# Windowed attention block on one core: row maxima on the full array, narrower score strips, and a deferred Q/K split

## The chip, the cores and the metric

The kernel runs on one core of one Trainium2 chip. The metric is the device time of one execution in microseconds; the median of the runs shown is compared. A core has TensorE (PE, with its weight loads shown as PEld), VectorE (DVE), ScalarE (ACT), GpSimd (POOL) and SyncE (SP, which issues nearly all transfers here). Each engine works off its own queue in order; the queues meet at semaphores.

## The reference, cut to what matters

The program computes one transformer block on a [2048, 640] input: a layer norm, sliding-window attention, and a gated MLP whose gate mixes over positions. Only the attention matters here.

```python
B, S, D = x.shape
H = 32; Dh = D // H; W = 256
qkv = (lambda x, *d: x.transpose(*d))((x @ wqkv).reshape(B, S, 3, H, Dh), 2, 0, 3, 1, 4)
q, k, v = qkv[0], qkv[1], qkv[2]
scores = jnp.einsum("bhqd,bhkd->bhqk", q, k) * (Dh ** -0.5)
idx = jnp.arange(S)
mask = (idx[:, None] - idx[None, :] >= 0) & (idx[:, None] - idx[None, :] < W)
scores = jnp.where(mask[None, None], scores, -1e9)
p = _softmax(scores, axis=-1)
o = jnp.einsum("bhqk,bhkd->bhqd", p, v)
```

A query sees itself and the 255 positions before it. The softmax needs each row's maximum, so the kernel computes the scores twice: once with queries on partitions, to take the maxima, and once with keys on partitions, for the exponentials.

## The kernel before, in words

**Tiles and stages.** The 2048 positions are 16 tiles of 128; the 32 heads are 8 groups g of 4 heads hh. The order of work on PE, DVE and ACT is the order in which the Python code emits it (manual schedule, lines 38-39). POOL and SP are placed by the framework's scheduler at build time, from the dependencies.

**Norm and V** (lines 463-485): for 16 tiles, load, normalise, transpose, and multiply for V. The normalisation takes two short POOL instructions (lines 75, 76) between its DVE steps. Before it, POOL fills constants: `mask` (lines 220-223) and `strip` (224-231), the additive masks of the maxima.

**Q and K** (lines 486-499): `qk_item(m, c)` makes 128 rows of Q/K for 512 positions: 15 matmuls of 512 columns (lines 434-436) into one of two PSUM banks, with a `yield` after every third. Then it splits the result into three bf16 pieces: ACT copies (440), DVE subtracts (441), ACT copies (442), POOL subtracts (443), and SP writes the pieces to `qk_d` in DRAM (446). Of 40 items 24 run back to back. `load_stack(g)` reads a group's pieces back into one of three slots; the pieces lie on the contraction axis, 120 rows deep.

**Lead** (lines 501-530): the other 16 items are drawn out of the generator `dense` three matmuls at a time (a dense step), and between them stand the maxima of group 0 (64 items) and of the first four query tiles of group 1 (16 items).

**`max_item(g, qb, hh)`** (lines 267-285) takes one of three PSUM banks (tag s1) and fills it with four matmuls side by side, each 32 queries (a strip) against the 288 keys that these 32 can see; for qb < 2 all four go against the first 128 or 256 keys. Then one fused DVE operation (284) adds the mask, reduces by max into a column of `mcol`, and writes the sums that nobody reads to `junk`, a bf16 tile of which there are two buffers. On the chip it is two DVE instructions: the reduction, and a read of the accumulator, which signals the end of the item. Ahead of the reduction stands a wait on DVE's own semaphore as an instruction of its own; the wait for PE is part of the reduction. `max_rows(g)` (287-299) turns a finished group's maxima with PE, splits them on DVE (292-296), and sends them through DRAM into the slot, as three rows more of Q.

**Attention steps** (lines 535-567): for s from 0 to 129 and hh from 0 to 3, in this order: the `max_item` 20 units ahead (while s < 108), the `score_item` of unit s, and, after hh = 2, `pv_item(s - 2)`. A unit is one group and one tile of 128 keys.

**`score_item`** (lines 317-341), while s <= 108, takes one of three PSUM banks (tag s2): four matmuls side by side, 32 keys each against the 384 queries from the tile's first on. ACT exponentiates the 384 columns into `pt` (335). After the fourth head POOL zeroes what lies outside the window: the triangle in the first 128 columns (337), that in the last 128 (340). From s = 109 on, items are two heads wide. `pv_item` (343-371) multiplies `pt` with V; every fourth unit a finished bank is copied out, by ACT (366) in most of the stage.

**The rest**: the output projection, and the MLP (lines 574-1105), which the change doesn't touch.

Of the kernel before, what the change touches and what calls it, by code (L numbers as in the profile page):

```python
# [7 lines left out]
F32 = mybir.dt.float32  # L8
F32R = mybir.dt.float32r
BF16 = mybir.dt.bfloat16  # L10
AF = mybir.ActivationFunctionType
OP = mybir.AluOpType
# [3 lines left out]
P = 128  # L16
# [11 lines left out]
NEG = -3.0e38  # L28
# [6 lines left out]
def block_kernel(ctx, tc, x, wqk, wv, wo, w_in, wsp, bsp, w_out, out):  # L35
    nc = tc.nc
# [4 lines left out]
    def pool(stack, name, **kw):  # L41
# [17 lines left out]
                            compare_op=OP.is_equal, fill=0.0)  # L59
# [138 lines left out]
    with ExitStack() as ab:  # L198
# [15 lines left out]
        def add_slot(i, flat):  # L214
# [2 lines left out]

        add_slot(0, slot0)
        add_slot(2, xb[:, :4 * S])
        mask = tmp2.tile([P, 256], BF16, name="mask")  # L220
        nc.gpsimd.memset(mask, 0.0)
        nc.gpsimd.affine_select(out=mask, in_=mask, pattern=[[-1, 256]], base=128, channel_multiplier=1,
                                compare_op=OP.is_ge, fill=NEG)
        strip = tmp2.tile([P, 288], BF16, name="strip")
        nc.gpsimd.memset(strip, 0.0)
        for j in range(4):
            m = strip[32 * j:32 * j + 32]
            nc.gpsimd.affine_select(out=m, in_=m, pattern=[[1, 288]], base=-1, channel_multiplier=-1,
                                    compare_op=OP.is_ge, fill=NEG)
            nc.gpsimd.affine_select(out=m, in_=m, pattern=[[-1, 288]], base=256, channel_multiplier=1,  # L230
                                    compare_op=OP.is_ge, fill=NEG)
        v_sb = vpool.tile([P, NT, VW], F32, name="v_sb")
        nc.gpsimd.memset(v_sb[:, :, 672:VW], 0.0)
        v4 = v_sb[:, :, :672].rearrange("p t (h c) -> p t h c", c=21)
# [2 lines left out]
        LEAD = 20  # L237
# [2 lines left out]
        psB = ab.enter_context(ExitStack())  # L240
        ps6 = [pool(psB, "ps6", space=PSUM)]

        def s1_tile(name):
            return ps6[0].tile([P, 512], F32, tag="s1", bufs=3, name=name)

        def s2_tile(name):
            return ps6[0].tile([P, 512], F32, tag="s2", bufs=3, name=name)

        def pv_tile(name):
            return psA.tile([P, 512], F32, tag="pv", bufs=2, name=name)  # L250
# [13 lines left out]
                    nc.sync.dma_start(st[j:6 * DH:6, a], src)  # L264
                    yield

        def max_item(g, qb, hh):

            st = slot_ap[g % 3]
            ps = s1_tile(f"sm{g}_{qb}_{hh}")  # L270
            if qb < 2:
                n, keep = (qb + 1) * P, mask[:, 256 - (qb + 1) * P:]
            else:
                n, keep = 288, strip
            for j in range(4):
                q0 = qb * P + 32 * j
                k0 = 0 if qb < 2 else q0 - 256
                nc.tensor.matmul(ps[32 * j:32 * j + 32, :n], st[:120, 0, hh, q0:q0 + 32], st[:120, 1, hh, k0:k0 + n],  # L278
                                 start=True, stop=True, tile_position=(0, 32 * j))
            if qb == 0 and hh == 0:  # L280
                m_cols[g] = tmp2.tile([P, 64], F32, tag="mcol", bufs=2, name=f"mcol{g}")
            junk = tmp2.tile([P, 288], BF16, tag="junk", bufs=2, name=f"junk{g}_{qb}_{hh}")
            c = hh * 16 + qb
            nc.vector.tensor_tensor_reduce(out=junk[:, :n], in0=ps[:, :n], in1=keep, scale=1.0,  # L284
                                           scalar=NEG, op0=OP.add, op1=OP.max, accum_out=m_cols[g][:, c:c + 1])
# [30 lines left out]

        def score_item(u, hh, width):

            g, kb = divmod(u, NT)
            st = slot_ap[g % 3]  # L320
            n = min(384, S - kb * P)
            if hh == 0:
                p_tiles[u] = tmp3.tile([P, 4, 384], F32, tag="pt", bufs=4, name=f"pt{u}")
            pt = p_tiles[u]
            if width == 1:
                ps = s2_tile(f"st{u}_{hh}")[:, None, :]
            else:
                ps = ps6[0].tile([P, 2, 512], F32, tag="sp", bufs=3, name=f"st{u}_{hh}")
            for j in range(width):
                for i in range(4):  # L330
                    k0 = kb * P + 32 * i
                    nc.tensor.matmul(ps[32 * i:32 * i + 32, j, :n], st[:123, 1, hh + j, k0:k0 + 32],  # L332
                                     st[:123, 0, hh + j, kb * P:kb * P + n], start=True, stop=True,
                                     tile_position=(0, 32 * i))
            nc.scalar.activation(pt[:, hh:hh + width, :n], ps[:, :, :n], AF.Exp, scale=SCALE)  # L335
            if hh + width == 4:
                nc.gpsimd.affine_select(out=pt[:, :, :P], in_=pt[:, :, :P], pattern=[[0, 4], [1, P]], base=0,  # L337
                                        channel_multiplier=-1, compare_op=OP.is_ge, fill=0.0)
                if n == 384:
                    nc.gpsimd.affine_select(out=pt[:, :, 256:], in_=pt[:, :, 256:], pattern=[[0, 4], [-1, P]],  # L340
                                            base=-1, channel_multiplier=1, compare_op=OP.is_ge, fill=0.0)
# [32 lines left out]
        if True:  # L374
# [26 lines left out]
            def vgemm(i):  # L401
                c, o = divmod(i, 4)
                t0 = o * P
                for j in range(2):
                    ps = (s1_tile if j else pv_tile)(f"v{i}_{j}")
                    n0 = j * HD
                    for k in range(KD):
                        hi, lo = xn_hi[c][:, k, t0:t0 + P], xn_lo[c][:, k, t0:t0 + P]
                        wh, wl = wv_hi[:, k, n0:n0 + HD], wv_lo[:, k, n0:n0 + HD]
                        nc.tensor.matmul(ps[:, :HD], hi, wh, start=(k == 0), stop=False)  # L410
                        nc.tensor.matmul(ps[:, :HD], hi, wl, start=False, stop=False)
                        nc.tensor.matmul(ps[:, :HD], lo, wh, start=False, stop=(k == KD - 1))
                    nc.scalar.activation(v4[:, i, 16 * j:16 * j + 16, :DH],
                                         ps[:, :HD].rearrange("p (h c) -> p h c", c=DH), AF.Copy)

            wqs, raws = {}, {}

            def load_wqk(m):
                raws[m] = tmp.tile([P, KD, P], F32, tag="wraw", bufs=5, name=f"wqraw{m}")
# [10 lines left out]
            def qk_item(m, c):  # L430
                ps = pv_tile(f"qk{m}_{c}")
                hi, lo = wqs[m]
                for k in range(KD):
                    nc.tensor.matmul(ps, hi[:, k, :], xn_hi[c][:, k, :], start=(k == 0), stop=False)
                    nc.tensor.matmul(ps, hi[:, k, :], xn_lo[c][:, k, :], start=False, stop=False)
                    nc.tensor.matmul(ps, lo[:, k, :], xn_hi[c][:, k, :], start=False, stop=(k == KD - 1))
                    yield
                sg = tmp.tile([P, 3, 512], BF16, tag="ta", bufs=3, name=f"sg{m}_{c}")
                rest = tmp.tile([P, 512], F32, tag="tb", bufs=2, name=f"rest{m}_{c}")
                nc.scalar.activation(sg[:, 0, :], ps, AF.Copy)  # L440
                nc.vector.tensor_tensor(out=rest, in0=ps, in1=sg[:, 0, :], op=OP.subtract)  # L441
                nc.scalar.activation(sg[:, 1, :], rest, AF.Copy)  # L442
                nc.gpsimd.tensor_tensor(out=sg[:, 2, :], in0=rest, in1=sg[:, 1, :], op=OP.subtract)  # L443
                T = S // 2
                base = qk_d[m // 5, 0, m % 5 * 8, 0, c * 256:(c + 1) * 256]
                nc.sync.dma_start(bass.AP(tensor=base.tensor, offset=base.offset,
                                          ap=[[T, P], [2 * DH * H // 2 * T, 3], [1, 256]]), sg.bitcast(F32))
# [23 lines left out]
            for i in range(NT):  # L471
                if i + 3 < NT:
                    load_x(i + 3)
                if i + 2 < NT:
                    ln1(i + 2)
                if i == 0:
                    vgemm(0)
                if i + 1 < NT:
                    turn1(i + 1)
                if i >= NT - 6 and i < NT - 2:  # L480
                    load_wqk(i - (NT - 6))
                if i >= NT - 3:
                    split_wqk(i - (NT - 3))
                if i:
                    vgemm(i)
            ld0, ld1 = load_stack(0), load_stack(1)
            for m in range(6):
                for c in range(4):
# [26 lines left out]
                next(dense, None)  # L515
            for u in range(16):
                for hh in range(4):
                    max_item(0, u, hh)
                    if hh < 3:
                        next(dense, None)  # L520
            max_rows(0)
            for u in range(LEAD - 16):
                for hh in range(4):
                    if u:
                        max_item(1, u - 1, hh)
                    next(dense, None)
            for hh in range(4):
                max_item(1, LEAD - 17, hh)
            for _ in dense:
                pass  # L530

        b1.close()
# [565 lines left out]
    n = NT - 2  # L1098
# [34 lines left out]
```

## Time and profile before

| | us |
|---|---|
| median of three runs | 1188.22 (1185.37 to 1189.32) |
| the profiled execution | 1185.69 |
| its span, first to last instruction | 1184.0 |
| PE busy | 1126.5 |
| DVE busy | 738.8 |
| ACT busy | 537.6 |
| POOL busy | 391.5 |

The span is what the trace covers; the profiled execution's own time is 1.7 us longer. Busy times count stretches in which an engine has at least one instruction under way; matmuls are pipelined, so a busy PE can still be a waiting one. The line numbers of the profile are those of the kernel above. In the tables, the columns after the count (x) are the busy time, the mean duration of one instruction, and the idle time of the engine just before such instructions with what ended it. Two instructions of an engine can overlap in the trace: what an instruction costs is then the distance from its start to the next start, which is shorter than its duration.

### The profile page before, as it was taken

How to read it: one execution, taken by the hardware profiler on the slowest of the kernel's cores; microseconds unless marked ns; L12 is line 12 of the kernel's file. 1: busy time of each engine (PE TensorE's matmuls, PEld its weight loads, DVE VectorE, ACT ScalarE, POOL GpSimd, SP SyncE). 2: the span in 40 equal slices, each digit the busy share in tenths (PEclk: the TensorE clock that was granted, in tenths of full speed). 3: DMA queues.
4: the chain of work that ended last, by engine and by line, in shares of the span. 5: the costliest groups of instructions: out<-in, count | busy, mean ns of one | idle time of the engine just before them, and what ended most of it. 6: DMA issues, size and time to landing. Idle time of an engine off the chain costs nothing. (4 is left out here: it accounts for less than half of the span.)

```text
span 1184.0 us, 26538 instructions
## 1 busy us (share of the span) xinstructions
PE 1126.5 (95%) x10272; PEld 963.8 (81%) x10272; DVE 738.8 (62%) x1949; ACT 537.6 (45%) x1121; POOL 391.5 (33%) x485
## 2 busy tenths in 40 slices
PE   5999999999999999878899999899999899999998
PEld 5998886546666666468899999799999889999998
DVE  5541123658888888559967658755548985656443
ACT  3333433228888888834446655433335531221110
POOL 4123443336556555845722036100015530000000
PEclk9999999999999999989999999899999999999999
DMA  6212453543444441558845441133331364444322
GB/s 191 77 34 89 143 195 138 187 150 114 173 166 175 174 175 42 188 174 289 270 156 189 174 134 36 36 132 131 120 139 57 125 193 152 129 140 136 86 87 82
DMA packets 72125, 165.20 MB, mean 140 GB/s; under 512 B 9128, under 2 KB 33448, under 8 KB 70056
## 3 DMA queue, kind: packets, MB, share of 16 engines
q1 hardware_dynamic: 69696, 158.27, 40.1%
q10 hardware_dynamic: 2304, 5.24, 1.1%
q8 instruction: 80, 1.31, 0.5%
q14 instruction: 45, 0.37, 0.1%
HBM read 108.83 MB, written 54.66 MB: 138 GB/s over the span
## 5 line engine op out<-in xcount | busy, mean ns | idle before, releaser
L335 ACT ACTIVATE pt<-st 128x384 f32<-128x384 f32 (+2 forms) x474 | 199.0, 513 | 34.8 <-PE st L332 27.3
L284 DVE CUSTOM_DVE_ANT_0 junk<-sm,strip 128x288 bf16<-128x288 f32 x448 | 181.0, 454 | 50.8 <-PE sm L278 49.6
L930 PE MATMUL g<-zl,aw 128*128 128x432 f32 x768 | 173.6, 361 | 7.2 <-ACT zl L598 4.9
L598 ACT ACTIVATE aw<-fx 128x512 fp32r<-128x512 f32 (+2 forms) x160 | 92.9, 596 | 185.7 <-PE g L930 120.9
L930 PEld LDWEIGHTS g<-zl,aw 128*128 128x128 f32 x768 | 144.6, 189 | 15.3 <-ACT zl L598 5.7
L930 PE MATMUL g<-ze,aw 128*128 128x432 f32 x576 | 137.0, 365 | 4.1 <-DVE row L592 1.8
L592 DVE TENSOR_TENSOR aw<-fx,aw 128x512 fp32r<-128x512 f32 (+2 forms) x152 | 108.4, 722 | 36.2 <-ACT aw L598 36.0
L930 PEld LDWEIGHTS g<-ze,aw 128*128 128x128 f32 x576 | 108.8, 192 | 11.6 <-ACT aw L598 1.7
L332 PE MATMUL st<-slot 123*32 123x384 bf16 (+2 forms) x1536 | 110.6, 318 | 6.6 <-ACT pt L335 3.6
L337 POOL TENSOR_SCALAR_AFFINE_SELECT pt<-pt 128x512 f32<-128x512 f32 x128 | 82.1, 642 | 90.9 <-ACT pt L335 90.9
L278 PE MATMUL sm<-slot 120*32 120x288 bf16 (+2 forms) x1536 | 109.1, 284 | 3.2 <-DVE mcol L284 2.5
L356 PE MATMUL pv<-pt,v_sb 128*32 128x384 f32 (+2 forms) x1408 | 102.7, 384 | 3.0 <-POOL pt L340 1.9
L969 PE MATMUL out_ps<-wout,y_sp 128*128 128x320 f32 (+1 forms) x630 | 96.2, 309 | 0.4 <-ACT y_sp L122 0.4
L834 PE MATMUL zb<-win,aw 128*128 128x432 f32 x480 | 95.3, 359 | 0.0
L969 PEld LDWEIGHTS out_ps<-wout,y_sp 128*128 128x128 f32 (+1 forms) x630 | 94.1, 188 | 1.2 <-ACT y_sp L122 0.7
L834 PEld LDWEIGHTS zb<-win,aw 128*128 128x128 f32 x480 | 89.9, 187 | 4.7
L278 PEld LDWEIGHTS <-slot 120*32 120x32 bf16 x1536 | 49.2, 95 | 42.6 <-issue 35.0
L332 PEld LDWEIGHTS <-slot 123*32 123x32 bf16 x1536 | 50.4, 96 | 38.3 <-issue 19.3
L441 DVE TENSOR_TENSOR rest<-qk,sg 128x512 f32<-128x512 f32 x40 | 27.7, 691 | 86.3 <-ACT sg L440 86.0
L443 POOL TENSOR_TENSOR sg<-rest,sg 128x512 bf16<-128x512 f32 x40 | 46.5, 1163 | 98.7 <-ACT sg L442 96.2
L340 POOL TENSOR_SCALAR_AFFINE_SELECT pt<-pt 128x512 f32<-128x512 f32 x112 | 73.9, 660 | 0.0
L592 DVE TENSOR_TENSOR row<-g,row 128x432 f32<-128x432 f32 x80 | 48.1, 604 | 36.0 <-PE g L930 32.3
(172 smaller groups left out, 2092.8 us busy)
## 6 DMA issues: line engine op xcount, KB each, us to landing
slot<-qk_d SPq DMA_DIRECT2D x72, 320.0 KB
fx<-wsp_in SPq DMA_DIRECT2D x32, 512.0 KB
qk_d<-sg SPq DMA_DIRECT2D x40, 384.0 KB
fx<-hn_d SPq DMA_DIRECT2D x32, 320.0 KB
o_d<-ot SPq DMA_DIRECT2D x32, 256.0 KB
xb<-qk_d SPq DMA_DIRECT2D x24, 320.0 KB
z_d<-row SPq DMA_DIRECT2D x16, 432.0 KB
g_d<-row SPq DMA_DIRECT2D x16, 432.0 KB
```

What stands on the lines that cost most here:

```text
L278: nc.tensor.matmul(ps[32 * j:32 * j + 32, :n], st[:120, 0, hh, q0:q0 + 32], st[:120, 1, hh, k0:k0 + n], start=True, stop=True, tile_positi ...
L284: nc.vector.tensor_tensor_reduce(out=junk[:, :n], in0=ps[:, :n], in1=keep, scale=1.0, scalar=NEG, op0=OP.add, op1=OP.max, accum_out=m_cols ...
L332: nc.tensor.matmul(ps[32 * i:32 * i + 32, j, :n], st[:123, 1, hh + j, k0:k0 + 32], st[:123, 0, hh + j, kb * P:kb * P + n], start=True, sto ...
L335: nc.scalar.activation(pt[:, hh:hh + width, :n], ps[:, :, :n], AF.Exp, scale=SCALE)
L337: nc.gpsimd.affine_select(out=pt[:, :, :P], in_=pt[:, :, :P], pattern=[[0, 4], [1, P]], base=0, channel_multiplier=-1, compare_op=OP.is_ge ...
L340: nc.gpsimd.affine_select(out=pt[:, :, 256:], in_=pt[:, :, 256:], pattern=[[0, 4], [-1, P]], base=-1, channel_multiplier=1, compare_op=OP. ...
L356: nc.tensor.matmul(ps[32 * hh:32 * hh + 32, a - 512 * c:b - 512 * c], v_sb[:, kb, v0:v0 + 32], pt[:, hh, a - kb * P:b - kb * P], start=fir ...
L592: (eng or nc.vector).tensor_tensor(out=out, in0=a, in1=b, op=op)
L598: nc.scalar.activation(out, a, AF.Copy)
L834: nc.tensor.matmul(b[0][:, :HF], a[t][:, x, kk], win2[0][:, y, kk, h * HF:(h + 1) * HF], start=kk + x + y == 0, stop=kk == KD - 1 and x == 1)
L930: nc.tensor.matmul(ps, w[m][:, x, k], zc[k][m][:, y], start=start and k + x + y == 0, stop=stop and k == 3 and x == 1, skip_group_check=True)
L969: nc.tensor.matmul(ps[j][:, :HD], src[:w, a, k, :], e1["wout"][:w, b, k, j * HD:(j + 1) * HD], start=(k == 0 and a + b == 0), stop=(k == K ...
```

## The change

- **Maxima.** `max_item` gets a flag. In the lead it is off, and a query tile from the third on is one matmul of 128 queries against 384 keys on the full array, in place of four strips of 288; the first two tiles are one matmul too, of 128 and 256 keys. In the attention steps the flag is on: the third tile and later ones keep the strips, the first two are one matmul. `mask` grows to 384 columns, with a second select for the window's far edge. `junk` grows to 384 columns and has one buffer in place of two.
- **Strip mask.** The code that builds `strip` moves from ahead of the norms to behind the V stage.
- **Scores.** The three score banks become fixed tiles that are taken in turn. An item that is one head wide computes, for each strip of 32 keys, the 288 queries that can see them and not all 384. ACT still reads 384 columns: what lies outside a strip's 288 is left from earlier uses of the bank, and the selects of lines 337 and 340 zero it.
- **Q/K split.** `qk_item` ends with the first ACT copy only. The DVE subtraction is emitted after the first three matmuls of the next item, the rest of the split after the second three; the last item's remainder after the last maxima of the lead.

```diff
@@ -217,18 +217,13 @@

         add_slot(0, slot0)
         add_slot(2, xb[:, :4 * S])
-        mask = tmp2.tile([P, 256], BF16, name="mask")
+        mask = tmp2.tile([P, 384], BF16, name="mask")
         nc.gpsimd.memset(mask, 0.0)
-        nc.gpsimd.affine_select(out=mask, in_=mask, pattern=[[-1, 256]], base=128, channel_multiplier=1,
+        nc.gpsimd.affine_select(out=mask, in_=mask, pattern=[[1, 384]], base=-1, channel_multiplier=-1,
+                                compare_op=OP.is_ge, fill=NEG)
+        nc.gpsimd.affine_select(out=mask, in_=mask, pattern=[[-1, 384]], base=256, channel_multiplier=1,
                                 compare_op=OP.is_ge, fill=NEG)
         strip = tmp2.tile([P, 288], BF16, name="strip")
-        nc.gpsimd.memset(strip, 0.0)
-        for j in range(4):
-            m = strip[32 * j:32 * j + 32]
-            nc.gpsimd.affine_select(out=m, in_=m, pattern=[[1, 288]], base=-1, channel_multiplier=-1,
-                                    compare_op=OP.is_ge, fill=NEG)
-            nc.gpsimd.affine_select(out=m, in_=m, pattern=[[-1, 288]], base=256, channel_multiplier=1,
-                                    compare_op=OP.is_ge, fill=NEG)
         v_sb = vpool.tile([P, NT, VW], F32, name="v_sb")
         nc.gpsimd.memset(v_sb[:, :, 672:VW], 0.0)
         v4 = v_sb[:, :, :672].rearrange("p t (h c) -> p t h c", c=21)
@@ -240,11 +235,14 @@
         psB = ab.enter_context(ExitStack())
         ps6 = [pool(psB, "ps6", space=PSUM)]

+        s2s, s2n = [ps6[0].tile([P, 512], F32, name=f"s2_{i}") for i in range(3)], [0]
+
         def s1_tile(name):
             return ps6[0].tile([P, 512], F32, tag="s1", bufs=3, name=name)

         def s2_tile(name):
-            return ps6[0].tile([P, 512], F32, tag="s2", bufs=3, name=name)
+            s2n[0] += 1
+            return s2s[s2n[0] % 3]

         def pv_tile(name):
             return psA.tile([P, 512], F32, tag="pv", bufs=2, name=name)
@@ -264,22 +262,26 @@
                     nc.sync.dma_start(st[j:6 * DH:6, a], src)
                     yield

-        def max_item(g, qb, hh):
+        def max_item(g, qb, hh, strips=True):

             st = slot_ap[g % 3]
             ps = s1_tile(f"sm{g}_{qb}_{hh}")
-            if qb < 2:
-                n, keep = (qb + 1) * P, mask[:, 256 - (qb + 1) * P:]
+            lo = max(0, qb - 2) * P
+            n = (qb + 1) * P - lo
+            if strips and qb > 1:
+                n, keep = 288, strip
+                for j in range(4):
+                    q0 = qb * P + 32 * j
+                    nc.tensor.matmul(ps[32 * j:32 * j + 32, :n], st[:120, 0, hh, q0:q0 + 32],
+                                     st[:120, 1, hh, lo + 32 * j:lo + 32 * j + n], start=True, stop=True,
+                                     tile_position=(0, 32 * j))
             else:
-                n, keep = 288, strip
-            for j in range(4):
-                q0 = qb * P + 32 * j
-                k0 = 0 if qb < 2 else q0 - 256
-                nc.tensor.matmul(ps[32 * j:32 * j + 32, :n], st[:120, 0, hh, q0:q0 + 32], st[:120, 1, hh, k0:k0 + n],
-                                 start=True, stop=True, tile_position=(0, 32 * j))
+                keep = mask[:, 384 - n:]
+                nc.tensor.matmul(ps[:, :n], st[:120, 0, hh, qb * P:(qb + 1) * P], st[:120, 1, hh, lo:lo + n],
+                                 start=True, stop=True)
             if qb == 0 and hh == 0:
                 m_cols[g] = tmp2.tile([P, 64], F32, tag="mcol", bufs=2, name=f"mcol{g}")
-            junk = tmp2.tile([P, 288], BF16, tag="junk", bufs=2, name=f"junk{g}_{qb}_{hh}")
+            junk = tmp2.tile([P, 384], BF16, tag="junk", bufs=1, name=f"junk{g}_{qb}_{hh}")
             c = hh * 16 + qb
             nc.vector.tensor_tensor_reduce(out=junk[:, :n], in0=ps[:, :n], in1=keep, scale=1.0,
                                            scalar=NEG, op0=OP.add, op1=OP.max, accum_out=m_cols[g][:, c:c + 1])
@@ -329,8 +332,9 @@
             for j in range(width):
                 for i in range(4):
                     k0 = kb * P + 32 * i
-                    nc.tensor.matmul(ps[32 * i:32 * i + 32, j, :n], st[:123, 1, hh + j, k0:k0 + 32],
-                                     st[:123, 0, hh + j, kb * P:kb * P + n], start=True, stop=True,
+                    b, e = (32 * i, min(n, 32 * i + 288)) if width == 1 else (0, n)
+                    nc.tensor.matmul(ps[32 * i:32 * i + 32, j, b:e], st[:123, 1, hh + j, k0:k0 + 32],
+                                     st[:123, 0, hh + j, kb * P + b:kb * P + e], start=True, stop=True,
                                      tile_position=(0, 32 * i))
             nc.scalar.activation(pt[:, hh:hh + width, :n], ps[:, :, :n], AF.Exp, scale=SCALE)
             if hh + width == 4:
@@ -413,7 +417,7 @@
                     nc.scalar.activation(v4[:, i, 16 * j:16 * j + 16, :DH],
                                          ps[:, :HD].rearrange("p (h c) -> p h c", c=DH), AF.Copy)

-            wqs, raws = {}, {}
+            wqs, raws, after = {}, {}, [iter(())]

             def load_wqk(m):
                 raws[m] = tmp.tile([P, KD, P], F32, tag="wraw", bufs=5, name=f"wqraw{m}")
@@ -434,11 +438,21 @@
                     nc.tensor.matmul(ps, hi[:, k, :], xn_hi[c][:, k, :], start=(k == 0), stop=False)
                     nc.tensor.matmul(ps, hi[:, k, :], xn_lo[c][:, k, :], start=False, stop=False)
                     nc.tensor.matmul(ps, lo[:, k, :], xn_hi[c][:, k, :], start=False, stop=(k == KD - 1))
+                    if k < 2:
+                        next(after[0], None)
                     yield
+                for _ in after[0]:
+                    pass
+                after[0] = split_qk(m, c, ps)
+                next(after[0])
+
+            def split_qk(m, c, ps):
                 sg = tmp.tile([P, 3, 512], BF16, tag="ta", bufs=3, name=f"sg{m}_{c}")
                 rest = tmp.tile([P, 512], F32, tag="tb", bufs=2, name=f"rest{m}_{c}")
                 nc.scalar.activation(sg[:, 0, :], ps, AF.Copy)
+                yield
                 nc.vector.tensor_tensor(out=rest, in0=ps, in1=sg[:, 0, :], op=OP.subtract)
+                yield
                 nc.scalar.activation(sg[:, 1, :], rest, AF.Copy)
                 nc.gpsimd.tensor_tensor(out=sg[:, 2, :], in0=rest, in1=sg[:, 1, :], op=OP.subtract)
                 T = S // 2
@@ -483,6 +497,13 @@
                     split_wqk(i - (NT - 3))
                 if i:
                     vgemm(i)
+            nc.gpsimd.memset(strip, 0.0)
+            for j in range(4):
+                m = strip[32 * j:32 * j + 32]
+                nc.gpsimd.affine_select(out=m, in_=m, pattern=[[1, 288]], base=-1, channel_multiplier=-1,
+                                        compare_op=OP.is_ge, fill=NEG)
+                nc.gpsimd.affine_select(out=m, in_=m, pattern=[[-1, 288]], base=256, channel_multiplier=1,
+                                        compare_op=OP.is_ge, fill=NEG)
             ld0, ld1 = load_stack(0), load_stack(1)
             for m in range(6):
                 for c in range(4):
@@ -515,18 +536,20 @@
                 next(dense, None)
             for u in range(16):
                 for hh in range(4):
-                    max_item(0, u, hh)
+                    max_item(0, u, hh, False)
                     if hh < 3:
                         next(dense, None)
             max_rows(0)
             for u in range(LEAD - 16):
                 for hh in range(4):
                     if u:
-                        max_item(1, u - 1, hh)
+                        max_item(1, u - 1, hh, False)
                     next(dense, None)
             for hh in range(4):
-                max_item(1, LEAD - 17, hh)
+                max_item(1, LEAD - 17, hh, False)
             for _ in dense:
+                pass
+            for _ in after[0]:
                 pass

         b1.close()
```

## The prediction, made blind

> **What bounds the kernel now.** I read the page first, then the busy times by stage, then single stretches of the timeline.
>
> ```profile
> span 1184.0 us, 26538 instructions
> ...
> L284 DVE CUSTOM_DVE_ANT_0 junk<-sm,strip 128x288 bf16<-128x288 f32 x448 | 181.0, 454 | 50.8 <-PE sm L278 49.6
> ```
>
> ```profile
> core 0: us, PE busy (x) PEld busy (x) DVE busy (x) ACT busy (x) POOL busy (x), PEclk, DMA share, GB/s
> 90.00:193.20 103.20, 102.70 (x457) 83.80 (x456) 18.68 (x27) 39.28 (x65) 47.22 (x36) 1.00 0.44 151
> 193.20:265.60 72.40, 70.42 (x518) 36.75 (x518) 42.60 (x176) 15.96 (x26) 21.25 (x15) 1.00 0.45 154
> 265.60:475.00 209.40, 200.54 (x4630) 133.77 (x4622) 176.08 (x890) 180.80 (x458) 124.52 (x203) 1.00 0.40 144
> ```
>
> The rows are the Q/K items, the lead, and the 108 attention steps with maxima. PE is all but full in the first two. In the third, DVE (176 of 209 us), ACT (181) and PE (201) are all close to the wall: a step takes 209.4 / 108 = 1.94 us, and whatever makes one of the three slower by a fifth becomes the bound. One step, on PE:
>
> ```profile
> 365.06 0.35 PE L332 MATMUL st<-slot 123*32 123x384 bf16 x4
> 365.23 0.31 PE L278 MATMUL sm<-slot 120*32 120x288 bf16 x4
> 365.35 0.35 PE L332 MATMUL st<-slot 123*32 123x384 bf16 x4
> 365.53 0.31 PE L278 MATMUL sm<-slot 120*32 120x288 bf16 x4
> 365.71 0.35 PE L332 MATMUL st<-slot 123*32 123x384 bf16 x4
> 365.87 0.84 PE L356 MATMUL pv<-pt,v_sb 128*32 128x256 f32 x16
> 366.52 0.31 PE L278 MATMUL sm<-slot 120*32 120x288 bf16 x4
> ```
>
> Read the distances of the starts: a group of score strips (384 columns) costs 0.17 us, a group of maxima strips (288) 0.12, the product with V 0.65. That is 1.80 a step; the rest are waits, as at 365.71, 0.06 late.
>
> **The one buffer of `junk`** is the part that decides. Before, maxima run back to back on DVE like this:
>
> ```profile
> 264.49 0.45 DVE L284 CUSTOM_DVE_ANT_0 junk<-sm,strip 128x288 bf16<-128x288 f32 x1
> 264.87 0.08 DVE L284 DVE_READ_ACCUMULATOR2_ANT mcol<- 128x1 f32 x1
> 264.87 0.45 DVE L284 CUSTOM_DVE_ANT_0 junk<-sm,strip 128x288 bf16<-128x288 f32 x1
> 265.25 0.08 DVE L284 DVE_READ_ACCUMULATOR2_ANT mcol<- 128x1 f32 x1
> ```
>
> An item costs 0.38 us: the next reduction starts together with the accumulator read of the last one. That is possible because, with two buffers, the wait in front of a reduction is for the accumulator read of the item before the last. In the changed program as built, the count waited for is one higher: the accumulator read of the very last item. The wait instructions are there already, so nothing new shows in an instruction count:
>
> ```profile
> L284 DVEq EVENT_SEMAPHORE  x496: 21/21/21, 194.6 to 473.9; - x166
> ```
>
> Now the parts follow each other. The accumulator read starts when the reduction is through, with a follower or without:
>
> ```profile
> 249.30 0.46 DVE L284 CUSTOM_DVE_ANT_0 junk<-sm,strip 128x288 bf16<-128x288 f32 x1 [0.66 <-PE sm L278]
> 249.69 0.08 DVE L284 DVE_READ_ACCUMULATOR2_ANT mcol<- 128x1 f32 x1
> 250.16 0.28 DVE L292 TENSOR_SCALAR m<-mt 64x128 bf16<-64x128 f32 x1 [0.39 <-PE mt L289]
> 250.48 0.28 DVE L293 SCALAR_TENSOR_TENSOR mr<-mt,m 64x128 f32<-64x128 f32 x1
> ```
>
> So 0.39 and 0.08, and then the way over the semaphore. Its price is not shown for this instruction. From below: L293 waits for L292 on the same engine and starts 0.04 after its end (250.16 + 0.28 to 250.48), with the wait inside the instruction. The wait here stands alone, as it does ahead of L441:
>
> ```profile
> 112.85 0.60 ACT L440 ACTIVATE sg<-qk 128x512 bf16<-128x512 f32 x1 [1.46 <-PE qk L436]
> ...
> 113.55 0.69 DVE L441 TENSOR_TENSOR rest<-qk,sg 128x512 f32<-128x512 f32 x1 [2.82 <-ACT sg L440]
> ```
>
> From the end of L440 (113.45) to L441 are 0.10. That is the nearest row, and I take it: 0.39 + 0.08 + 0.10, **0.57 us an item**; by the lower price it would be 0.51. Four items make 2.28 us a step. PE then needs 4 x 0.12 + 4 x 0.12 + 0.65 = 1.6, ACT 180.8 / 108 = 1.7, POOL 1.2: DVE alone sets the step, and the columns saved on PE buy nothing. The three banks hide nothing, as they only let PE run ahead of DVE.
>
> A rule of the Trainium skill speaks against this: VectorE: DVE Perf Modes, section "The DRAIN you can't avoid", measured the same time for eight copies with a semaphore after each as with one after the last, and says that the semaphore costs nothing extra, since the next operation waits for an empty pipe anyhow. By it an item would stay at 0.38 us. The rows at 264.49 disagree as far as they go: a reduction recorded at 0.45 is followed after 0.38, so there is an overlap that a wait can take away.
>
> The other widths come from one row of the view of `junk`:
>
> ```profile
> L284 DVE CUSTOM_DVE_ANT_0 junk<-sm,mask x64: 275/354/427, 193.5 to 447.1; 128x128 bf16<-128x128 f32 x32, 128x256 bf16<-128x256 f32 x32
> ```
>
> The shortest is 128 wide, the longest 256. Less the 0.07 of overlap, plus 0.19 for read and wait (0.57 - 0.38): 0.40 and 0.54; at 0.14 per 128 columns, 0.67 for 384. The steps hold 48 items of group 1 and six groups of 64 (4 of 0.40, 4 of 0.54, 56 of 0.57, which is 35.7) with a `max_rows` of 1.2 each (250.16 on, four operations): 27.4 + 6 x 36.9 = 248.7 us on DVE, without a gap. They take 209.4 now: **+39.3**.
>
> **The lead.** PE, where a single item stands between dense steps, and one round of four items and three dense steps:
>
> ```profile
> 200.74 0.40 PE L436 MATMUL qk<-xa,wql 128*128 128x512 f32 x1
> 201.07 0.31 PE L278 MATMUL sm<-slot 120*32 120x288 bf16 x4
> 201.30 0.50 PE L434 MATMUL qk<-xa,wqh 128*128 128x512 f32 x1
> 201.64 0.40 PE L435 MATMUL qk<-xa,wqh 128*128 128x512 f32 x1
> 201.88 0.40 PE L436 MATMUL qk<-xa,wql 128*128 128x512 f32 x1
> ...
> 204.59 0.31 PE L278 MATMUL sm<-slot 120*32 120x288 bf16 x4
> ```
>
> Dense matmuls follow after 0.24. The item adds 0.33 + 0.23 + 0.34 - 2 x 0.24 = 0.42, though its columns take 0.12: going into strips and out of them costs 0.1 each way. That agrees with the Trainium skill's TensorEngine Tiling (Array Packing), Key Properties: a change of tiling mode drains the array. A matmul on the full array should cost its 384 columns, 0.17 by the score groups. That is not shown for a bf16 matmul among these; from the other side it may cost the same 0.42. I take 0.17, as the strips' own columns cost no more elsewhere. A round, now 3.52 (201.07 to 204.59), would need 3 x 0.71 + 4 x 0.17 = 2.8 on PE. But DVE needs 4 x 0.67, plus 0.6 of an L441 (0.69, of which 0.42 counts, as it fills a wait): 2.93. Fourteen rounds save 14 x 0.59 = 8.3. The 16 narrower items among dense steps save 0.25 each: 4.0. At the end eight items of 384 columns follow each other on DVE: 8 x (0.67 - 0.38), less 0.2 where L441 fills a wait, loses 2.1; and the last split now comes behind them all, so that the first exponential, which takes over its buffers, is late: 0.7, an estimate. Sum: **-9.5**. If full-array items cost what strips do, it is +2.5.
>
> **The start.** The strip mask isn't built later in effect: the order of the built program has POOL's eight selects of `strip` ahead of the first L76, as before. `mask` adds work there, and the first transposes wait for it:
>
> ```profile
> 1.59 0.29 POOL L58 TENSOR_SCALAR_AFFINE_SELECT ident<-ident 128x128 f32<-128x128 f32 x1
> 1.84 0.40 POOL L222 TENSOR_SCALAR_AFFINE_SELECT mask<-mask 128x256 bf16<-128x256 bf16 x1
> ```
> ```profile
> L76 POOL TENSOR_TENSOR mva<-mva,half x1: 573/573/573, 9.5 to 9.5; 128x1 f32<-128x1 f32 x1
> L79 DVE TENSOR_SCALAR xn<-xt,mva x1: 614/614/614, 10.1 to 10.1; 128x640 f32<-128x640 f32 x1
> ```
>
> Two selects of 0.51 (0.11 per 128 columns) for one of 0.40, and a wider memset, 0.1: **+0.7**; nothing if L79 has slack.
>
> **The deferred split** I cost at nothing. It changes no PE instruction; PE is full for 102.70 of the 103.20 us of these items and hides the chain behind it, which has two banks. In the worst case ACT's six weight copies, now ahead of the second ACT copy, each delay a bank by their length, about 0.7: +4. Fixed score banks are waited for as the rotating ones were: nothing.
>
> **Sum.** 1185.7 (the profiled execution, span 1184.0) + 39.3 - 9.5 + 0.7 = 1216.2. That execution lies 2.5 under the median of 1188.2, so I say **1217**.
>
> **Rivals.**
> - *The wait is free* (13%). DVE stays under the wall. The lead is then bound by PE: 14 x 0.73 + 4.0, less some 0.7 at its end, saves 13.5. In the steps the fourth score group still waits for the exponential that frees its bank (365.71); its own loop shrinks by the 0.04 that 96 columns take, and the group by 0.04 more: 0.08 in some 11 of 16 steps, the others bound by ACT's copies: 108 x 11/16 x 0.08 = 6. 1185.7 - 13.5 - 6 + 0.7 = **1167**. It decides if an item stays under 1.94 / 4 = 0.48 us. The Trainium skill's section named above would have it so. Against it stands the overlap at 264.49.
> - *Half the price* (6%): 0.51 an item, with the wait's way at 0.04. Six groups of 33.1 and 48 x 0.51 make 223, +13.5; the lead, then bound by PE, saves 11.8: **1188**, within 0.3%.
> - *Full-array items are no cheaper* (9%): **1228**. For it: bf16 beside f32 weights is not shown. Against it: the drain sits at the change of tiling.
> - *The forecast* (72%).
>
> **Numbers.** 0.3% is about what a measurement of this kernel tells from no change. The third rival's 9% and the forecast lie in 1204 to 1231; 19% are left out. Faster by over 0.3%: 13% and 2 of the 6; the same 3%; slower 82%.
>
> **What would show it.** Starts of reductions 0.57 apart in the steps with the accumulator read in the gap; DVE's time in L284 unchanged but PE waiting for `mcol`; steps of 2.28 us. In the lead, no 0.1 on either side of an item, and PE waiting for DVE. Reductions still 0.38 apart would refute the forecast.

## The result, and the profile after

The changed kernel takes **1235.15 us** (median of four runs, 1234.25 to 1237.88) against 1187.36 before (median of four, three of which are those of the table above): slower, by a factor of **1.041** (95% interval 1.038 to 1.043). The direction and the mechanism were forecast; the time lies 18 us above the forecast and 4 above the end of its range. The profiled execution took 1234.56, its span 1232.2.

The page, and the busy times by stage (same columns as before; the stages run from the first maxima item to the first of the attention steps, and from there to the last maxima):

```profile
span 1232.2 us, 25780 instructions
...
L286 DVE CUSTOM_DVE_ANT_0 junk<-sm,strip 128x288 bf16<-128x288 f32 x384 | 175.9, 458 | 57.1 <-PE s L336 1.5
```

```profile
193.20:258.70 65.50, 59.90 (x287) 36.24 (x286) 50.23 (x177) 15.32 (x25) 21.11 (x15) 0.99 0.49 173
258.70:524.50 265.80, 225.39 (x4474) 130.08 (x4469) 201.99 (x888) 206.45 (x461) 125.12 (x204) 0.99 0.31 113
```

The lead is shorter (65.2 us from first reduction to first reduction, 72.1 before), the steps are longer (265.4, 208.9 before), and what follows the last maxima is 1.4 shorter: -7.0 + 56.5 - 1.4 and 0.1 ahead of the lead make the 48.2 of the spans.

In the group of L286 look at the idle time before the reductions: 57.1 us, of which the page puts no more than 1.5 down to PE, the largest cause that it names (before: 49.6 of 50.8). The timeline of DVE in the steps shows what nearly all the rest is:

```profile
360.21 0.46 DVE L286 CUSTOM_DVE_ANT_0 junk<-sm,strip 128x288 bf16<-128x288 f32 x1
360.60 0.08 DVE L286 DVE_READ_ACCUMULATOR2_ANT mcol<- 128x1 f32 x1
360.82 0.46 DVE L286 CUSTOM_DVE_ANT_0 junk<-sm,strip 128x288 bf16<-128x288 f32 x1
361.21 0.08 DVE L286 DVE_READ_ACCUMULATOR2_ANT mcol<- 128x1 f32 x1
```

The accumulator read no longer starts together with the next reduction: it ends at 360.68, then 0.14 us pass, and the next one starts. An item costs 0.61, and 384 times 0.14 are 54 us. PE, which had been the fullest engine, now waits for DVE. These are its largest waits in the steps (total us, times, longest), first the one for DVE as it was in the kernel before, from 270 to 460 us:

```profile
PE sm L278 <- DVE mcol L284: 2.1, 6, 0.4
```
```profile
PE sm L275 <- DVE mcol L286: 34.2, 184, 0.3
PE s L336 <- ACT pt L339: 1.7, 1, 1.7
```

In the lead the item itself is as cheap on PE as forecast:

```profile
224.06 0.40 PE L440 MATMUL qk<-xb,wql 128*128 128x512 f32 x1
224.30 0.34 PE L280 MATMUL sm<-slot 120*128 120x384 bf16 x1
224.34 0.53 PE L438 MATMUL qk<-xb,wqh 128*128 128x512 f32 x1
224.71 0.40 PE L439 MATMUL qk<-xb,wqh 128*128 128x512 f32 x1
...
225.75 0.32 PE L280 MATMUL sm<-slot 120*128 120x384 bf16 x1 [0.24 <-DVE mcol L286]
```

The distances around it add to 0.24 + 0.04 + 0.37 = 0.65, against 0.48 without an item: 0.17, where a strip item had added 0.42. The last row shows the other side: PE waits for DVE here too.

### The profile page after: what moved, and what is told of

Its sections match the earlier page's. It is cut to its first block, busy times and chain, and to the rows that moved or that the text cites. A ratio compares the mean times of both kernels' runs of the same rounds, so it can differ in the third digit from the quotient of the medians.

```text
span 1232.2 us, 25780 instructions
## 1 busy us (share of the span) xinstructions
PE 1138.7 (92%) x9888; PEld 957.8 (78%) x9888; DVE 771.9 (63%) x1949; ACT 561.6 (46%) x1121; POOL 393.0 (32%) x486
## 5 line engine op out<-in xcount | busy, mean ns | idle before, releaser
L339 ACT ACTIVATE pt<-s 128x384 f32<-128x384 f32 (+2 forms) x436 | 196.2, 473 | 59.9 <-PE s L336 43.9
L286 DVE CUSTOM_DVE_ANT_0 junk<-sm,strip 128x288 bf16<-128x288 f32 x384 | 175.9, 458 | 57.1 <-PE s L336 1.5
L275 PE MATMUL sm<-slot 120*32 120x288 bf16 x1088 | 84.6, 296 | 25.6 <-DVE mcol L286 24.7
L336 PE MATMUL s<-slot 123*32 123x288 bf16 (+4 forms) x1232 | 93.9, 286 | 1.7 <-ACT pt L339 1.7
L286 DVE CUSTOM_DVE_ANT_0 junk<-sm,mask 128x384 bf16<-128x384 f32 (+2 forms) x128 | 58.4, 457 | 20.4 <-PE sm L280 6.0
```

The source lines that it names most:

```text
L336: nc.tensor.matmul(ps[32 * i:32 * i + 32, j, b:e], st[:123, 1, hh + j, k0:k0 + 32], st[:123, 0, hh + j, kb * P + b:kb * P + e], start=True ...
```

## The experiments

Theory: the single buffer of `junk` makes each maxima item wait for the one just before it, and this alone is the loss; the other parts gain. Rivals: the fixed banks, the strips or the deferred split lose the time; or PE's columns count more or less than forecast. Each kernel is compared with the kernel before on the same chip.

**1. Two buffers in the changed kernel.**

```diff
-            junk = tmp2.tile([P, 384], BF16, tag="junk", bufs=1, name=f"junk{g}_{qb}_{hh}")
+            junk = tmp2.tile([P, 384], BF16, tag="junk", bufs=2, name=f"junk{g}_{qb}_{hh}")
...
-            mr = tmp2.tile([64, P], F32, tag="mr", bufs=2, name=f"mr{g}")
+            mr = tmp2.tile([64, P], F32, tag="mr", bufs=1, name=f"mr{g}")
```

The second edit makes room in the core's memory for the first.

> The changed kernel with two buffers of junk (and one of mr in place of two, for the room). Theory: one buffer makes each maxima item wait for the accumulator read of the item just before, 0.61 us in place of 0.38, and that alone is the loss; with two buffers the other parts gain, 1165 to 1178 us, items 0.38 apart on DVE. Rival: the fixed score banks, the narrower strips or the deferred split lose the time, and DVE's waits only follow from that: it stays at 1225 or more.

Measured: 1177.03 us, ratio to the kernel before 0.991 (0.989 to 0.993): as the theory has it. Items are 0.38 apart again:

```profile
300.47 0.08 DVE L286 DVE_READ_ACCUMULATOR2_ANT mcol<- 128x1 f32 x1
300.47 0.46 DVE L286 CUSTOM_DVE_ANT_0 junk<-sm,strip 128x288 bf16<-128x288 f32 x1
300.85 0.08 DVE L286 DVE_READ_ACCUMULATOR2_ANT mcol<- 128x1 f32 x1
300.85 0.45 DVE L286 CUSTOM_DVE_ANT_0 junk<-sm,strip 128x288 bf16<-128x288 f32 x1
```

One buffer costs the changed kernel 58 us (1235.15 less 1177.03).

**2. One buffer in the kernel before**, nothing else (`bufs=2` to `bufs=1` in line 282).

> The kernel before with one buffer of junk and nothing else. Theory: items 0.61 us apart in the steps (four of them 2.44 us a step, 265 us for the 108 steps against 209), the lead bound by PE as before but for its last items: 1240 to 1248 us, more than the whole change costs. Rival: the single buffer costs nothing by itself, 1187 us.

Measured: 1244.54 us, ratio 1.048 (1.046 to 1.049), inside the theory's range. The same distances with the old code around them:

```profile
359.86 0.46 DVE L284 CUSTOM_DVE_ANT_0 junk<-sm,strip 128x288 bf16<-128x288 f32 x1
360.24 0.08 DVE L284 DVE_READ_ACCUMULATOR2_ANT mcol<- 128x1 f32 x1
360.47 0.46 DVE L284 CUSTOM_DVE_ANT_0 junk<-sm,strip 128x288 bf16<-128x288 f32 x1
```

The two together leave the rivals on banks, strips and split without a part in the loss: the buffer alone brings it, and its undoing removes it.

**3. Full score columns beside two buffers** (change 1, and):

```diff
-                    b, e = (32 * i, min(n, 32 * i + 288)) if width == 1 else (0, n)
+                    b, e = 0, n
```

> The first of these kernels with 384 score columns per strip again, fixed banks kept. Theory: the narrower strips give 0.08 us in 11 of 16 steps, so this one is about 6 us slower than the first. Rival: PE's columns are the bound in the steps and the strips give 0.16 us in each of 108 steps, 17 us. Third: nothing, since ACT sets the steps.

Measured: 1183.31 us, 6.3 above kernel 1 on the same chip, as the theory has it. Plain steps are 1.87 us here and 1.79 in kernel 1, steps with ACT's copy 2.02 in both.

**4. The same edit with one buffer kept.**

> The changed kernel, one buffer of junk kept, with 384 score columns a strip again. Theory: DVE sets the step with 0.61 us an item, so the narrower strips buy nothing while the one buffer stands: 1234 to 1237 us, as the changed kernel. Rival: PE's columns still count beside DVE, and this one is 6 us or more slower.

Measured: 1236.42 us (1234.08 to 1238.35), the changed kernel's time. While the one buffer stands, the narrower strips buy nothing that can be measured. PE shows how they are lost; the steps of this kernel, whose maxima are taken as in the changed one:

```profile
259.00:524.60 265.60, 235.68 (x4474) 130.64 (x4469) 201.71 (x888) 205.03 (x460) 124.84 (x204) 0.99 0.31 113
```

PE is busy 235.7 us, 10 more than in the changed kernel, in a stage of the same length.

**5. Narrow scores alone in the kernel before** (the diff's fixed banks and its `b, e`).

> The kernel before with the fixed score banks and 288 score columns a strip alone. Theory: plain steps go from 1.87 to 1.79 us, those with ACT's copy stay at 2.02: 6 us faster, 1180. Rival: nothing, ACT sets the steps; or 17, if PE's columns count in full.

Measured: 1180.75 us, ratio 0.996 (0.994 to 0.999), 5.8 us faster, with plain steps of 1.79. Kernels 1 and 3 and this one agree on 6 us for this part.

**6. No deferral, beside two buffers** (change 1, and):

```diff
-                    if k < 2:
-                        next(after[0], None)
                     yield
-                for _ in after[0]:
-                    pass
-                after[0] = split_qk(m, c, ps)
-                next(after[0])
+                for _ in split_qk(m, c, ps):
+                    pass
```

> The first of these kernels with the whole Q/K split emitted at the end of its own item, as before the change. Theory: the deferral is worth nothing, within 1.5 us of the first kernel. Rival: it keeps PE from waiting for a bank in the lead, where DVE is now busier, and this one is 3 us or more slower.

Measured: 1173.91 us (1173.10 to 1174.44; kernel 1: 1174.99 to 1178.28). Neither expectation holds: without the deferral it is 3.1 faster. A difference shows at the end of the lead. ACT in kernel 1, where the last split comes behind all maxima:

```profile
250.12 0.60 ACT L452 ACTIVATE sg<-qk 128x512 bf16<-128x512 f32 x1 [2.06 <-PE qk L440]
254.80 0.63 ACT L456 ACTIVATE sg<-rest 128x512 bf16<-128x512 f32 x1 [4.08 <-DVE rest L454]
256.75 1.64 ACT L339 ACTIVATE pt<-s 128x384 f32<-128x384 f32 x4 [1.32 <-POOL sg L457]
```

The first exponential waits for POOL's part of that split and starts 2.06 us after the steps' first reduction (254.69). Without the deferral it starts 0.16 after it (256.33 after 256.17), though it still waits for POOL:

```profile
256.33 2.14 ACT L339 ACTIVATE pt<-s 128x384 f32<-128x384 f32 x5 [2.76 <-POOL sg L453]
```

The steps take 207.1 in place of 209.1, which would be 2.0 of the 3.1. That the late exponential is the cause is likely but not shown: kernel 6 profiled once more (below) starts it 0.17 after the first reduction and has steps of 205.3, so two executions of one kernel differ by nearly as much.

**7. Strips in the lead, beside two buffers** (change 1, and `False` removed from the three calls of `max_item` in the lead).

> The changed kernel with two buffers of junk, and the lead's maxima from the third query tile on as strips of 288 again (the first two tiles stay one matmul). Theory: a full-array item saves the change of tiling on both sides, so the lead is 9 to 11 us longer here, 1186 to 1188 us. Rival: the change of tiling costs nothing and only the columns count; then strips are no worse, 1177.

Measured: 1184.28 us, 7.3 above kernel 1, measured on another chip (ratios to the kernel before 0.998 and 0.991, so 0.7%, 8 us). The lead is 68.5 us, in kernel 1 it is 61.4. The full array is worth 7 us in the lead, less than the 9 to 11 expected; the rival, that only columns count, does not hold.

**8. Strips for the first two query tiles in the steps** (kernel 6, and in `max_item`):

```diff
-            if strips and qb > 1:
-                n, keep = 288, strip
+            if strips:
+                n, keep = (288, strip) if qb > 1 else (n, mask[:, 384 - n:])
                 for j in range(4):
                     q0 = qb * P + 32 * j
+                    k0 = lo + 32 * j if qb > 1 else 0
```

> Two buffers of junk, no deferral, and in the attention steps strips for the first two query tiles as well, so that no full-array matmul stands among strips there; the lead keeps the full array. Theory: a full-array item among strips pays the change of tiling that it saves in the lead; the two steps in question take 4.84 us in place of 4.26 in each of seven groups, so this one is about 4 us faster than the kernel without deferral (1173.9): 1169 to 1171. Rival: these steps are long because of their scores' place, no gain.

Measured: 1173.72 us (1171.12 to 1177.19), ratio 0.989 (0.987 to 0.991), as kernel 6 (0.988). As the two had run on different chips, both ran once more on one chip:

> Two buffers of junk and no deferral, once more, on one chip with the kernel that also has strips for the first two query tiles in the steps. Theory: 1174, and 2 to 4 us slower than that kernel. Rival: no difference beyond 1 us, since what the two steps gain is lost again elsewhere.

> The same with strips for the first two query tiles in the steps. Theory: two steps in each group take 4.2 us in place of 4.8, 4 us in all, 1170. Rival: 1174, because the steps that follow wait longer for the transfer of the group's maxima, or for nothing that the profile shows.

Measured: 1172.79 (kernel 6) and 1172.88: no difference, as the rivals have it, and not the gain of 2 to 4 us. The local effect is there. In kernel 1 (POOL's first select, one in each step):

```profile
341.35 0.64 POOL L341 TENSOR_SCALAR_AFFINE_SELECT pt<-pt 128x512 f32<-128x512 f32 x1 [0.57 <-ACT pt L339]
343.72 0.64 POOL L341 TENSOR_SCALAR_AFFINE_SELECT pt<-pt 128x512 f32<-128x512 f32 x1 [1.15 <-ACT pt L339]
346.18 0.64 POOL L341 TENSOR_SCALAR_AFFINE_SELECT pt<-pt 128x512 f32<-128x512 f32 x1 [1.23 <-ACT pt L339]
```

and in kernel 8, the same steps:

```profile
341.85 0.63 POOL L342 TENSOR_SCALAR_AFFINE_SELECT pt<-pt 128x512 f32<-128x512 f32 x1 [0.57 <-ACT pt L340]
343.73 0.64 POOL L342 TENSOR_SCALAR_AFFINE_SELECT pt<-pt 128x512 f32<-128x512 f32 x1 [0.66 <-ACT pt L340]
346.06 0.64 POOL L342 TENSOR_SCALAR_AFFINE_SELECT pt<-pt 128x512 f32<-128x512 f32 x1 [1.11 <-ACT pt L340]
```

4.83 us become 4.21, and so in all six groups; kernel 6 has the 4.83 too. But of that, 3.7 us in all, nothing remains over the whole stage in the first pair of profiles (207.1 from first to last reduction in both), 1.5 in the second (205.3 and 203.7), and nothing in the time. Later steps are longer in places, some of them before the transfer of a group's maxima has landed, some with PE waiting for nothing that the profile shows. Which of these takes the gain back stays open.

**9. A plain add in place of the fused reduction, one buffer** (the kernel before; the maxima are left out, their columns zeroed once a group):

```diff
+                nc.vector.memset(m_cols[g], 0.0)
-            junk = tmp2.tile([P, 288], BF16, tag="junk", bufs=2, name=f"junk{g}_{qb}_{hh}")
+            junk = tmp2.tile([P, 288], BF16, tag="junk", bufs=1, name=f"junk{g}_{qb}_{hh}")
...
-            nc.vector.tensor_tensor_reduce(out=junk[:, :n], in0=ps[:, :n], in1=keep, scale=1.0,
-                                           scalar=NEG, op0=OP.add, op1=OP.max, accum_out=m_cols[g][:, c:c + 1])
+            nc.vector.tensor_tensor(out=junk[:, :n], in0=ps[:, :n], in1=keep, op=OP.add)
```

> The kernel before with one buffer of junk and a plain add of scores and mask in place of the fused reduction; the maxima are left out (their columns are zeroed once a group). It measures the way from the end of one DVE operation to the start of the next that waits for it through a wait instruction of its own. Theory A: the way is 0.10 us for a plain operation, as ahead of the subtraction of the Q/K split, and the 0.14 seen ahead of the reduction belongs to the fused operation. Theory B: it is 0.14 whenever the wait is for DVE's own end.

Measured: 1220.81 us in its one run. Four adds in a row, merged by the view:

```profile
360.09 2.15 DVE L285 TENSOR_TENSOR junk<-sm,strip 128x288 bf16<-128x288 f32 x4
```

An add takes 0.46, so starts are (2.15 - 0.46) / 3 = 0.56 apart: 0.10 from end to start. Theory A holds: ahead of a plain operation the way is 0.10, ahead of the fused reduction 0.14. What comes before differs too, an add here and an accumulator read there, but the traces have the wait instruction as well: in both kernels it ends 0.06 after the end of what it waits for. From there the add starts after 0.04 and the reduction after 0.08, so the difference lies at the start of the reduction. Why is not shown.

## Why the prediction was wrong

**The price of an item on DVE.** This is the step that failed. The chain (reduction, read, wait, next reduction) was right, and its first two terms measured 0.38 to 0.39 and 0.08. The last, "That is the nearest row, and I take it", was taken from L441, a plain subtraction that waits for ACT, at 0.10; it is 0.14, and an item costs 0.61, not 0.57. Kernel 9 shows that a plain operation that waits for DVE itself has the 0.10 too. So the row was near in form (a wait as an instruction of its own) but not the same operation. 0.04 us in each of the 431 intervals of the steps make 17, and the steps came out at +56.5, not +39.3. That this is the whole difference is in part luck: each `max_rows` added 0.9 and not 1.2, some 2 us less in all, and about as much went into a few waits for PE, where none were forecast. The working had no bound above 0.10 for this way, though no row showed it for the fused reduction; the range failed there.

**The lead.** Forecast -9.5, measured -7.0. Most of the difference is the same 0.04. The rounds of four items are bound by DVE, as forecast, at 2.84 us (4 x 0.71) without a subtraction and mostly 3.21 with one: 3.06 on average, not 2.93, which is 1.9 in 14 rounds, and the eight items at the end add 0.3. Two smaller misses work against each other: the 16 items among dense steps saved 2.8, not 4.0, and the 0.7 for the late exponential falls behind the lead.

PE's side was right: 0.17 an item, as taken. The 0.1 on each side of an item is gone at 224.30, and in the steps of kernel 1 it is back, where full-array items stand among strips:

```profile
342.75 0.31 PE L336 MATMUL s<-xb 123*32 123x288 bf16 x4
342.99 0.28 PE L280 MATMUL sm<-slot 120*128 120x256 bf16 x1
343.20 0.31 PE L336 MATMUL s<-xb 123*32 123x288 bf16 x4
```

The strips take 0.24 to the next start here and 0.12 among strips. That agrees with the rule of the Trainium skill that a change of tiling mode drains the array (TensorEngine Tiling (Array Packing), Key Properties).

**Scores, deferral, start.** That the columns saved on PE buy nothing beside a DVE at the wall is shown by kernel 4. The deferral, costed at nothing but for the late first exponential at 0.7, costs 3 us with two buffers (kernel 6); what it costs with one was not tried. At the start L76 moved as forecast in kind:

```profile
L76 POOL TENSOR_TENSOR mva<-mva,half x1: 573/573/573, 10.0 to 10.0; 128x1 f32<-128x1 f32 x1
```

It is 0.5 later, not 0.7, and at the first maxima 0.05 of it is left (193.56 after 193.51); between there are 180 us of other work, which differ by about 1 us from kernel to kernel.

**The rivals.** "The wait is free" does not hold: kernels 1 and 2 price it at 58 and 59 us. The Trainium skill's statement that the semaphore costs nothing extra, measured there on eight copies (VectorE: DVE Perf Modes, "The DRAIN you can't avoid"), does not hold for these items, whose distance goes from 0.38 to 0.61 us. "Half the price", 0.51 an item, does not hold either, nor does "Full-array items are no cheaper", by kernel 7.

What the first rival would have given, 1167, can be held against kernel 1, where the wait is gone: 1177. Its lead saved 10.7, not 13.5; its steps nothing, not 6. The narrower scores by themselves are worth the 6 (kernel 5), so something takes them back. Two candidates show, neither proven in the time: the full-array items among strips lengthen two steps of each group by 0.6 in all (kernel 8), a part of the change that the prediction did not price at all; and the first exponential comes 2 us late (kernel 6).

**The best version** is kernel 6 or 8, without a difference between them: the change with two buffers and without the deferral, about 1173, 1.1 to 1.2% faster than before.

## What to carry to other kernels

A scratch output that nobody reads still orders the instructions that write it: with one buffer each writer waits for the one before, on its own engine, and the overlap between them is gone. Look in the built program at what each wait counts up to, not only at how many waits there are, and multiply by the items of the stage whose engines are all near the wall. If a price must come from another row, take it from the same operation, or widen the range by what the operation may add.

## What the runs showed of the hardware

Two fused reductions in a row start 0.38 us apart when the second waits for the item before the last, and 0.61 when it waits for the last one (the changed kernel beside kernel 1, kernel 2 beside the kernel before). A wait for DVE's own last result, as an instruction of its own, lets the next operation start 0.10 us after the end if it is a plain add (kernel 9) and 0.14 if it is the fused reduction (changed kernel and kernel 2). A bf16 matmul of 384 columns on the full array between f32 matmuls of 512 adds 0.17 us in the changed kernel, what 384 columns take among strips; the same item as strips of 288 added 0.42 in the kernel before. With PE waiting 34 us for DVE in the steps, its granted clock stayed at 0.99.
